# Padding of 64 bytes behind each row of the second weight matrix and each activation buffer, in a fused convolution and two-layer MLP on one core

## The chip, the core and the metric

The kernel runs on one core of a Trainium2 chip. The core has a matrix engine (TensorE, PE in the profile; PEld is its loading of weights), a vector engine (VectorE, DVE), a scalar engine (ScalarE, ACT), GpSimd (POOL) and a queue engine that starts transfers (SyncE, SP). They run side by side and wait for each other by semaphores. On-chip memory has 128 partitions, each of them a row of bytes; an address below means the byte within a partition. The metric is the device time of one execution in microseconds.

## The reference

```python
w = softmax(weight_gen, axis=-1)               # (4, 4096, 8 heads, 7 taps)
x = sum over k of w[..., k] * x_padded[s + k]  # causal, 7 taps, per head of 24 channels: (16384, 192)
h = x @ w_in                                   # (16384, 192) @ (192, 2048)
g = where(h >= 1, h, where(h <= -1, 0, (h + 1) ** 2 / 4))
out = g @ w_out                                # (16384, 2048) @ (2048, 192)
```

All inputs and the output are float32.

## The kernel before

The 16384 tokens are worked in 32 blocks of 512. For each block GpSimd and VectorE compute the convolution, and its result is turned so that channels lie on partitions. Then the block goes through the two matrix products: `steps` lists all (block, f) with f from 0 to 15, f being a slice of 128 of the 2048 hidden channels, and the main loop takes them two at a time (a pair, `w`), 8 pairs a block, 256 in all.

To keep float32 precision each operand of a product is held as a high and a low part in a reduced float32 type (F32R): `hc` and `hl` for the convolution's result, `whi` and `wlo` for the first matrix, `gh` and `gl` for the hidden values; `wo` holds for each f the high and then the low part of 128 rows of the second matrix, 192 columns each.

`gemm1_pair` computes a pair's two slices of h. `relu`, `square` (ScalarE) and `act_g` (VectorE) make g in place, and `split_g` (L398 to L405) writes gh on ScalarE (L403) and gl on VectorE (L404), each into one of six buffers of 512 words. `gemm2_part` follows two pairs later (`LAGP = 2`), in two parts per pair: it loads 128 columns of gh as weights and streams the 384 words of wo's row (high and low part together), then loads the same columns of gl and streams the 192 words of the high part alone (L432). Both products use the array as two halves of 64 rows each: the half is `h` in the code, and the matmul of one half runs beside that of the other. One turn of the loop so issues nine steps of the first product (each with both halves) and eight steps of the second, a step being gh and then gl for both halves.

The order on every engine is the order in which the code is written (`tc.manual_schedule()`). In the first pairs the weights are decoded and split: `high` (ScalarE, L352) and `low` (VectorE, L356) write `whi`, `wlo` and the two parts of `wo`, which `views` returns.

The built program places, in bytes within a partition: `whi` at 17408, `wlo` at 29696, `wo` at 41984 with a row every 1536, the gh buffers from 151552 on and the gl buffers from 163840 on with one every 2048, and behind them the convolution's `piece` buffers, the output buffers `osb` and the raw weights `r`. All starts of wo's rows, of gh, gl, hc, hl, whi and wlo, and of the 128-column slices of gh and gl that are loaded as weights, are multiples of 512. A `piece` has rows of 1024 bytes; its 128-column slices, which are loaded as weights where it is turned (L267), begin at 0, 256 and 512 within a row.

Of the kernel before, what the change touches and what calls it, by code (L numbers as in the profile page):

```python
# [11 lines left out]
F32R = mybir.dt.float32r  # L12
# [10 lines left out]
def kernel(  # L23
# [22 lines left out]
    P = 128  # L46
    B, S, D = x.shape
# [5 lines left out]
    NF = DFF // P  # L53
# [21 lines left out]
    const = ctx.enter_context(tc.tile_pool(name="const", bufs=1))  # L75
# [6 lines left out]
    gp = ctx.enter_context(tc.tile_pool(name="gp", bufs=6))  # L82
# [11 lines left out]
    warm = const.tile([P, 32], F32, tag="warm", name="warm")  # L94
    whi = const.tile([P, NF // 2, NC, P], F32R, tag="whi", name="whi")
    wlo = const.tile([P, NF // 2, NC, P], F32R, tag="wlo", name="wlo")
    wo = const.tile([P, NF, 2, D], F32R, tag="wo", name="wo")
    heads = [const.tile([P, (D // Q) * P + 2 * D + 0, 2], U16, tag=f"head{m}", name="head") for m in range(2)]

    def run(ops):  # L100
# [297 lines left out]

    def split_g(i):
        gv = h_t.pop(i)[:, 0:N]  # L400
        gh = gp.tile([P, 512], F32R, tag="gh", name="gh")
        gl = gp.tile([P, 512], F32R, tag="gl", name="gl")
        nc.scalar.activation(out=gh[:, 0:N], in_=gv, func=AF.Copy)  # L403
        nc.vector.tensor_tensor(out=gl[:, 0:N], in0=gv, in1=gh[:, 0:N].bitcast(F32), op=ALU.subtract)  # L404
        g_t[i] = (gh, gl)  # L405
# [125 lines left out]
    with tc.manual_schedule():  # L531
# [55 lines left out]
        def first_pairs():  # L587
# [26 lines left out]
            low(2, 1)  # L614
            act_g(1)
            split_g(0)
            relu(2)
            square(2)
            split_g(1)
            relu(3)  # L620
            square(3)
            act_g(2)
            act_g(3)
            split_g(2)
            split_g(3)
            cast_act(3, 0)
# [123 lines left out]
```

## Time and profile before

| | |
|---|---|
| time, median of 2 runs | 1147.0 us (1146.97 to 1147.03) |
| the profiled execution | 1147.49 us, span of its instructions 1145.6 us |
| TensorE matmul (PE) | 1130.8 us busy, 12885 instructions |
| TensorE weight load (PEld) | 1053.4 us busy |
| ScalarE (ACT) | 964.4 us busy |
| VectorE (DVE) | 833.7 us busy |
| GpSimd (POOL) | 792.3 us busy |
| mean granted clock of TensorE | 0.996 of full speed |

Matmuls are pipelined: the record of one lasts longer than the distance to the next, and the two halves overlap, so the distance between starts tells what one costs. In a timeline, records that follow each other with the same line and tiles are merged into one row with their count (x2: the two halves), the first one's start and the length to the last one's end.

### The profile page before, as it was taken

The page shows a single profiled execution, that of the slowest core. Times are in us where ns is not written, and L with a number is a line of the kernel's source. Part 1 is how long each engine was busy: PE and PEld are TensorE (multiplying, and loading weights), DVE is VectorE, ACT ScalarE, POOL GpSimd, SP SyncE. Part 2 cuts the span into 40 slices and gives each one's busy share as a digit, 9 for nine tenths or more (in the row PEclk, how much of TensorE's full clock was granted, in tenths as well). Part 3 has the DMA queues.
Part 4 walks back from the last instruction along what each step waited for, and adds up shares of the span by engine and source line. Part 5 has one row for each costly group of instructions (what it writes and reads, how often), then busy time and mean ns, then how long its engine had stood idle before and what let it go on. Part 6 is the DMA issues. An engine that isn't in the chain of part 4 may idle for free.

```text
span 1145.6 us, 32197 instructions
## 1 busy us (share of the span) xinstructions
PE 1130.8 (99%) x12885; PEld 1053.4 (92%) x12885; DVE 833.7 (73%) x1271; ACT 964.4 (84%) x1745; POOL 792.3 (69%) x511
## 2 busy tenths in 40 slices
PE   7999999999999999999999999999999999999998
PEld 5889899999999999999999999999999999999997
DVE  8887767777676777767777677776767777677765
ACT  5878888888888888888888888888888888888886
POOL 4697976786866688486685866778576784866310
PEclk9899999999999999999999999999999999999999
DMA  9422222121222222222121222222222122221100
GB/s 231 113 77 75 88 86 92 62 84 66 80 91 91 65 82 67 78 99 91 57 82 67 86 91 87 64 77 76 78 91 79 67 81 76 83 91 57 48 24 16
DMA packets 84053, 91.44 MB, mean 80 GB/s; under 512 B 5056, under 2 KB 75712, under 8 KB 83904
## 3 DMA queue, kind: packets, MB, share of 16 engines
q1 hardware_dynamic: 83904, 89.39, 24.4%
q8 instruction: 102, 1.67, 0.6%
q14 instruction: 47, 0.39, 0.1%
HBM read 64.99 MB, written 24.38 MB: 78 GB/s over the span
## 4 chain that ended last, share of the span: by engine, by line
PE 90%; ACT 4%; DVE 2%; POOL 2%; issue 1%; DMA 1%; SPq 0%; DVEq 0%; POOLq 0%; ACTq 0%
PE o L432 46%; PE psh L378 44%; ACT u L392 1%; ACT u L389 1%; POOL acc L189 1%; DVE psh L397 1%; ACT gh L403 1%; PE psx L267 1%; DMA x<-in_x_dram 1%; POOL pr L179 1%; DVE gl L404 0%; ACT hc L258 0%; DVE s L153 0%; DVE psw L340 0%; ACT whi L352 0%
## 5 line engine op out<-in xcount | busy, mean ns | idle before, releaser
L432 PE MATMUL o<-wo,gh 64*128 64x384 f32 x4096 | 616.5, 353 | 0.8 <-SPq L441 0.8
L397 DVE SCALAR_TENSOR_TENSOR psh<-u,psh 128x512 f32<-128x512 f32 x512 | 354.7, 696 | 284.9 <-ACT u L392 284.6
L432 PE MATMUL o<-wo,gl 64*128 64x192 f32 x4096 | 560.8, 247 | 0.0
L432 PEld LDWEIGHTS o<-wo,gh 64*128 64x128 f32 x4096 | 472.8, 184 | 9.0 <-SPq L441 1.0
L432 PEld LDWEIGHTS o<-wo,gl 64*128 64x128 f32 x4096 | 468.7, 188 | 5.5
L378 PE MATMUL psh<-hc,whi 64*128 64x512 f32 x1536 | 371.4, 397 | 4.2 <-DVE wlo L356 2.5
L389 ACT ACTIVATE u<-psh 128x512 f32<-128x512 f32 x512 | 301.2, 588 | 79.7 <-PE psh L378 78.5
L378 PE MATMUL psh<-hc,wlo 64*128 64x512 f32 x1536 | 364.5, 390 | 0.0
L378 PE MATMUL psh<-hl,whi 64*128 64x512 f32 x1536 | 363.3, 389 | 0.0
L404 DVE TENSOR_TENSOR gl<-psh,gh 128x512 fp32r<-128x512 f32 x512 | 345.8, 686 | 15.2 <-ACT gh L403 1.1
L403 ACT ACTIVATE gh<-psh 128x512 fp32r<-128x512 f32 x512 | 299.2, 592 | 66.1 <-DVE psh L397 66.1
L189 POOL TENSOR_TENSOR acc<-acc,pr 128x768 f32<-128x768 f32 x185 | 343.5, 1857 | 6.6 <-DVE head L331 2.9
L392 ACT ACTIVATE u<-u 128x512 f32<-128x512 f32 x512 | 324.2, 633 | 16.0
L179 POOL TENSOR_TENSOR pr<-x,w 128x768 f32<-128x768 f32 x186 | 286.6, 1549 | 7.0 <-DVE psw L340 7.0
L259 POOL TENSOR_TENSOR hl<-XT,hc 128x512 fp32r<-128x512 f32 x90 | 115.2, 1293 | 209.9 <-ACT hc L258 146.8
L378 PEld LDWEIGHTS psh<-hc,whi 64*128 64x128 f32 x1536 | 200.3, 185 | 24.4 <-DVE wlo L356 4.1
L378 PEld LDWEIGHTS psh<-hl,whi 64*128 64x128 f32 x1536 | 200.1, 185 | 23.7 <-DVE hl L259 0.3
L378 PEld LDWEIGHTS psh<-hc,wlo 64*128 64x128 f32 x1536 | 200.3, 186 | 15.8
L179 POOL TENSOR_TENSOR acc<-x,w 128x768 f32<-128x768 f32 x31 | 48.1, 1551 | 69.9 <-DVE w L155 68.0
L258 ACT ACTIVATE hc<-XT 128x512 fp32r<-128x512 f32 x90 | 55.5, 618 | 0.0
L284 DVE STREAM_TRANSPOSE T<-acc 128x768 f32<-128x768 f32 x30 | 50.3, 1678 | 0.7 <-POOL acc L189 0.5
L457 DVE SCALAR_TENSOR_TENSOR osb<-o,osb 128x384 f32<-128x384 f32 x64 | 32.7, 555 | 2.6 <-ACT osb L456 2.6
(44 smaller groups left out, 188.0 us busy)
## 6 DMA issues: line engine op xcount, KB each, us to landing
x<-in_x_dram SPq DMA_DIRECT2D x28, 960.0 KB
XT<-D SPq DMA_DIRECT2D x180, 128.0 KB
out_dram<-osb SPq DMA_DIRECT2D x31, 384.0 KB
D<-T SPq DMA_DIRECT2D x30, 384.0 KB
x<-in_x_dram SPq DMA_DIRECT2D x4, 945.0 KB
w<-in_weight_gen_dram SPq DMA_DIRECT2D x15, 224.0 KB
r<-in_moe_w_in_dram SPq DMA_DIRECT2D x16, 192.0 KB
r<-in_moe_w_out_dram SPq DMA_DIRECT2D x8, 384.0 KB
```

Of the source, the lines that this page charges most:

```text
L179: held(eng.tensor_tensor(out=t, in0=xtile[:, k:k + n, :].rearrange("p j (h g) -> p j h g", h=H), in1=wt[:, gi, :, :, k:k + 1].to_broadcast ...
L189: held(eng.tensor_tensor(out=o, in0=s, in1=t, op=ALU.add))
L258: ops.append(lambda c=c: nc.scalar.activation(out=hc[:, c], in_=src[c], func=AF.Copy))
L259: ops.append(lambda c=c: lows.append(engines[c].tensor_tensor(out=hl[:, c], in0=src[c], in1=hc[:, c].bitcast(F32), op=ALU.subtract)))
L284: lambda: nc.vector.transpose(out=T.rearrange("p b c j -> p b j c"), in_=acc.rearrange("p j (r b) -> p b j r", b=R)),
L378: nc.tensor.matmul(out=pair[h][:, 0:N], lhsT=l[rows, f // 2, (c + h) % NC if b < 2 else c], rhs=r[rows, c], start=(s == 0), stop=(s == len ...
L389: nc.scalar.activation(out=u_t[i], in_=h_t[i][:, 0:N], func=AF.Relu, scale=0.5 * UNIT, bias=0.5)
L392: nc.scalar.activation(out=u_t[i], in_=u_t[i], func=AF.Square, scale=UNIT ** -0.5)
L397: nc.vector.scalar_tensor_tensor(out=pv, in0=uv, scalar=1.0 / UNIT, in1=pv, op0=ALU.min, op1=ALU.max)
L403: nc.scalar.activation(out=gh[:, 0:N], in_=gv, func=AF.Copy)
L404: nc.vector.tensor_tensor(out=gl[:, 0:N], in0=gv, in1=gh[:, 0:N].bitcast(F32), op=ALU.subtract)
L432: mm = nc.tensor.matmul(out=o_t[b][turn][:, k, 0:cols], lhsT=g_t[i][l][rows, t * P:(t + 1) * P], rhs=wo[rows, f].rearrange("p s d -> p (s ...
```

## The change

wo gets rows of 400 words, of which the first 384 are used as before; gh and gl get buffers of 528 words, of which the first 512 are used.

```diff
-    wo = const.tile([P, NF, 2, D], F32R, tag="wo", name="wo")
+    wo = const.tile([P, NF, 2 * D + 16], F32R, tag="wo", name="wo")[:, :, 0:2 * D].rearrange("p f (s d) -> p f s d", s=2)
...
-        gh = gp.tile([P, 512], F32R, tag="gh", name="gh")
-        gl = gp.tile([P, 512], F32R, tag="gl", name="gl")
+        gh = gp.tile([P, 512 + 16], F32R, tag="gh", name="gh")[:, 0:512]
+        gl = gp.tile([P, 512 + 16], F32R, tag="gl", name="gl")[:, 0:512]
```

The built programs have the same instructions in the same order on every engine, with the same waits and the same element counts; they differ in addresses alone, and in the row distance in the access patterns of the sixteen instructions that write the two parts of wo. wo's rows are now 1600 bytes apart and begin at multiples of 64, the gh and gl buffers are 2112 bytes apart. Tiles behind wo move up by 1024 bytes, those behind gl by 1792, which puts `piece`, `osb` and `r` 256 bytes further within 512.

## Rows read from the trace of the kernel before

**Rows 1.** The page: span, and busy time of each engine with its share and instructions.
```profile
span 1145.6 us, 32197 instructions
PE 1130.8 (99%) x12885; PEld 1053.4 (92%) x12885; DVE 833.7 (73%) x1271; ACT 964.4 (84%) x1745; POOL 792.3 (69%) x511
```

**Rows 2.** Stretches by window: from:to, length, busy time per engine, clock, DMA.
```profile
400.00:600.00 200.00, 200.00 (x2312) 196.94 (x2311) 145.64 (x221) 171.52 (x310) 152.35 (x97) 1.00 0.24 79
600.00:800.00 200.00, 200.00 (x2310) 182.99 (x2308) 145.37 (x219) 171.43 (x310) 145.79 (x94) 1.00 0.23 77
```

**Rows 3.** Waits of PE, longest and shortest of eight: total us, times, longest.
```profile
PE psx L208 <- POOL ident L541: 2.7, 1, 2.7
...
PE psh L378 <- DVE gl L404: 0.4, 2, 0.3
```

**Rows 4.** Timeline of PE, one turn: start, length, line, operation, tiles, shape, count.
```profile
601.63 0.33 PE L432 MATMUL o<-wo,gh 64*128 64x384 f32 x2
601.80 0.25 PE L432 MATMUL o<-wo,gl 64*128 64x192 f32 x2
601.89 0.36 PE L432 MATMUL o<-wo,gh 64*128 64x384 f32 x2
602.09 0.25 PE L432 MATMUL o<-wo,gl 64*128 64x192 f32 x2
602.17 0.36 PE L432 MATMUL o<-wo,gh 64*128 64x384 f32 x2
...
603.88 0.41 PE L378 MATMUL psh<-hc,whi 64*128 64x512 f32 x2
604.13 0.40 PE L378 MATMUL psh<-hc,wlo 64*128 64x512 f32 x2
...
605.73 0.39 PE L378 MATMUL psh<-hl,whi 64*128 64x512 f32 x2
605.96 0.33 PE L432 MATMUL o<-wo,gh 64*128 64x384 f32 x2
```

**Rows 5.** Timeline of the weight loads in the same turn.
```profile
601.41 0.19 PEld L432 LDWEIGHTS o<-wo,gh 64*128 64x128 f32 x2
601.63 0.19 PEld L432 LDWEIGHTS o<-wo,gl 64*128 64x128 f32 x2
601.80 0.19 PEld L432 LDWEIGHTS o<-wo,gh 64*128 64x128 f32 x2
601.91 0.19 PEld L432 LDWEIGHTS o<-wo,gl 64*128 64x128 f32 x2
```

**Rows 6.** Timeline of PE, second product 100 us later, other rows and buffers.
```profile
701.14 0.33 PE L432 MATMUL o<-wo,gh 64*128 64x384 f32 x2
...
701.69 0.36 PE L432 MATMUL o<-wo,gh 64*128 64x384 f32 x2
701.88 0.25 PE L432 MATMUL o<-wo,gl 64*128 64x192 f32 x2
...
703.39 0.41 PE L378 MATMUL psh<-hc,whi 64*128 64x512 f32 x2
```

**Rows 7.** Line L432, all of it: duration ns minimum/median/maximum, first and last start.
```profile
L432 PEld LDWEIGHTS o<-wo,gh x4096: 182/184/332, 25.7 to 1140.0; 64*128 64x128 f32 x196
L432 PE MATMUL o<-wo,gh x4096: 329/355/576, 26.0 to 1140.2; 64*128 64x384 f32 x196
L432 PEld LDWEIGHTS o<-wo,gl x4096: 183/188/334, 26.0 to 1140.6; 64*128 64x128 f32 x196
L432 PE MATMUL o<-wo,gl x4096: 243/247/362, 26.1 to 1140.7; 64*128 64x192 f32 x196
```

**Rows 8.** Line L267, the turning of the pieces, in the same columns.
```profile
L267 PEld LDWEIGHTS psx<-ident,piece x72: 137/140/142, 9.1 to 58.9; 128*128 128x128 f32 x72
```

**Rows 9.** Lines L403, L404, L352 and L356, in the same columns.
```profile
L403 ACT ACTIVATE gh<-psh x512: 576/598/612, 23.4 to 1137.3; 128x512 fp32r<-128x512 f32 x171
L404 DVE TENSOR_TENSOR gl<-psh,gh x512: 634/685/722, 24.5 to 1138.0; 128x512 fp32r<-128x512 f32 x171
L352 ACT ACTIVATE whi<-psw x8: 485/490/492, 14.3 to 51.4; 128x384 fp32r<-128x384 f32 x8
L352 ACT ACTIVATE wo<-psw x8: 472/492/499, 19.7 to 51.8; 128x384 fp32r<-128x384 f32 x8
L356 DVE TENSOR_TENSOR wlo<-psw,whi x8: 495/558/559, 15.1 to 51.9; 128x384 fp32r<-128x384 f32 x8
L356 DVE TENSOR_TENSOR wo<-psw,wo x8: 547/549/558, 20.2 to 52.4; 128x384 fp32r<-128x384 f32 x8
```

**Rows 10.** Stretches of the start by window, columns as in rows 2.
```profile
6.50:30.40 23.90, 18.44 (x151) 14.37 (x149) 21.89 (x40) 15.85 (x33) 10.30 (x8) 1.00 1.05 241
30.40:37.30 6.90, 6.50 (x36) 5.58 (x38) 5.88 (x12) 5.68 (x12) 4.69 (x3) 0.51 1.08 218
37.30:60.00 22.70, 21.61 (x224) 18.42 (x223) 19.56 (x36) 19.92 (x40) 16.64 (x10) 1.00 0.18 59
```

## The prediction, made before the result was known

> **What bounds the kernel now.** I read the page first. TensorE is busy for 1130.8 of 1145.6 us, far more than ScalarE (964.4) or VectorE (833.7) [rows 1]. A busy share alone doesn't say that TensorE waits for nobody, so I went on to the stretches by window: from 400 to 600 and from 600 to 800 us it is busy for 200.00 of 200.00 us at a granted clock of 1.00, while ScalarE has work for 171.5 and VectorE for 145.5 of each 200 us [rows 2]. The waits say the same: TensorE's longest wait by total is 2.7 us, and its wait for gl, the last thing made before the second matmul, is 0.4 us in all, in two places [rows 3]. So from about 60 us to the end the time is the length of TensorE's own queue, and an edit counts only as far as it changes what TensorE does per instruction.
>
> The timeline of TensorE shows what one turn of the main loop is made of [rows 4]. A row stands for two matmuls, one per half of 64 rows, and the second half runs along with the first, so what one costs is the distance from one row's start to the next. The first product takes nine steps: from 603.88 to 605.96, 2.08 us, mostly 0.23 us each. The second takes eight steps of one gh and one gl: from 601.63 to 603.88, 2.25 us. The turn is 601.63 to 605.96, 4.33 us. There are 32 blocks x 8 pairs = 256 turns: 256 x 4.33 = 1108 us of the 1145.6, and the second product, the part that reads the changed buffers, holds 256 x 2.25 = 576 us of it, in 256 x 8 = 2048 steps.
>
> Inside a step there is one thing that is not arithmetic. The first gh of a turn takes 0.17 us (601.63 to 601.80), the next ones 0.20 (601.89 to 602.09). The weight loads tell why [rows 5]: the load for the first gh starts at 601.41, 0.22 us ahead of its matmul. The load for the second starts at 601.80 together with the matmul of gl, and the next load follows at 601.91, so that load lasted 0.11 us, but the gl matmul has only 0.09 us of work to hide it. The seven later steps are (603.88 - 601.89) / 7 = 0.284 us long against 0.17 + 0.09 = 0.26 for the first: 0.025 us in each of the seven are a wait for a weight load.
>
> **The change part by part.** No instruction is added, removed, reordered or given another wait; every shape is the old one. What is left is addresses. Before, wo's rows are 1536 bytes apart and the twelve gh and gl buffers 2048 bytes, and all of them, and every slice of 128 columns that is loaded as weights, begin at a multiple of 512 bytes. After, rows and buffers are 64 bytes further apart each, so their starts are spread over the multiples of 64; what lies behind gl moves too (the raw weights, the pieces of the convolution and the output buffers now begin 256 bytes off a multiple of 512). Each of four kinds of work could notice:
>
> 1. TensorE's reads of wo, gh and gl, 2048 steps. Does their time hang on the address? The trace has two tests. First, wo's sixteen rows, the six gh and six gl buffers and the four slices lie at different distances from each other in every turn, in steps of 512 bytes, and two turns 100 us apart with other rows and other buffers repeat each other: 703.39 - 701.14 = 2.25 us, with a gh in the middle at 701.88 - 701.69 = 0.19 us, as before within the rounding of the rows [rows 6]. Over the 4096 matmuls of a kind, the median record is 355 ns for gh and 247 for gl with minima of 329 and 243; the loads have a median of 184 and 188 ns and a minimum of 182 and 183 [rows 7]. Second, an operand that is 256 bytes off: the convolution's pieces are loaded as weights in slices that begin 0, 256 and 512 bytes into a 1024-byte row, and all 72 of those loads last 137 to 142 ns [rows 8]; a third of them begin 256 bytes off, and no group stands apart by more than 5 ns. A step of 64 bytes is not in the trace. From below: if the whole 0.025 us wait were a collision of the load with the streaming read, and the padding ended it, 7 x 256 x 0.025 = 45 us would go. From above: the spread between kinds of loads in rows 7 is 188 - 184 = 4 ns, and between the two ends of rows 8 5 ns; if a read that begins off a multiple of 512 paid 5 ns for the load and 5 for the streaming, that would be 2048 x 0.010 = 20 us. I take 0, because rows 6 and 8 are the nearest and neither shows a dependence. A further reason: a load walks through 512 bytes in 0.11 us while the matmul walks through 768 or 1536 bytes in 0.09 or 0.17, so the two streams slide past each other over every offset in each step, wherever they begin. A collision by address would be met in every step before and after.
>
> The Trainium skill ("TensorE: Matmul & The Clock Gate", section "LDWEIGHTS (loading the stationary operand)") gives a weight load by its columns alone, columns over 1.2 GHz: 107 ns for 128. The 0.11 us between the two loads of rows 5 agrees with it, and by that rule the 0.025 us wait is the length of the load and no padding can take it away. The same skill ("SBUF — State Buffer", section "Who interferes with whom") gives TensorE two independent read ports and knows of one contention alone, that of VectorE with GpSimd; by it the sum is 0 too, where the collision reading gives minus 45 us.
>
> 2. The writes of gh by ScalarE (median 598 ns, 576 to 612) and of gl by VectorE (685, 634 to 722) [rows 9]: the same element count, contiguous, in another place. They are hidden: ScalarE has 200 - 171.5 = 28.5 us free in 200, VectorE 54.5 [rows 2], which at 200 / 4.33 = 46 turns is 0.62 and 1.18 us in each turn. With two gh and two gl per turn, a gh would have to grow by 0.31 us and a gl by 0.59 before TensorE waited. Without that cover, 10 ns on each would be 512 x 0.010 = 5 us.
>
> 3. The splitting of the weights into wo's two parts, eight instructions on each engine in the first 53 us. Here the row distance stands in the access pattern (400 words for 384). Its nearest row is the same instruction on the first matrix, where the output is contiguous: 490 ns against 492 on ScalarE, 558 against 549 on VectorE [rows 9]. A jump between rows costs nothing that shows; 16 x 0.01 us = 0.2 us at the most. I take 0.
>
> 4. Transfers and other engines on the moved tiles: sizes, counts and queues are the same. In the loop nobody on TensorE's side waits for them [rows 3]. I take 0.
>
> The sum: 1145.6 us of span + 0, and the profiled execution's 1147.5 us is 1.9 more than its span. It lies 0.5 us above the median of the runs, so the prediction is the median: 1147.0 us.
>
> One thing can move without any cause in the change. From 30.4 to 37.3 us the granted clock is 0.51, the lower level of 1.2 GHz; TensorE was busy for 18.4 of the 23.9 us ahead of it and for 21.6 of the 22.7 behind it, at 1.00 on both sides [rows 10]. The stretch costs about half its length, 3.5 us. Whether it comes, and how often, hangs on the first 40 us, where transfers and decoding race. Lost or doubled, it makes 1143.5 or 1150.5.
>
> **The rivals.** *Collisions end.* The streaming read of wo and the load of gh or gl lie on the same offsets, and the spread ends the 0.025 us waits: 1147 - 45 = 1102 us. For it: the wait is there, it is in the very part that is padded, and all starts share one alignment. Against it: 0.11 us is also the load's length where it waits for nothing, and rows 6 and 8 know no offset. If half of the collisions went, it would be 1124 us, just 2%.
>
> *Reads off the old alignment are dearer.* Every load and every stream now runs over one more boundary of 512 bytes than before; at 10 ns a step that is 1147 + 20 = 1167 us. It decides from 23 us / 2048 = 11 ns per step on (4% of the 284 ns), in the second product alone; at half the price it would be 1157 us and still within 2%. Against it stands rows 8, where a load that crosses such a boundary lasts as long as the others.
>
> *The start goes another way.* The change leaves the loop alone and the stretch of lower clock is lost or doubled, by the 3.5 us above: 1143.5 or 1150.5 us. For it: those 6.9 us lie where TensorE still waits for others, so a small shift can move them. Against it: the two runs of before lie 0.06 us apart, so the start repeats itself. That the padding does nothing is no rival here but the forecast.
>
> **How the numbers follow.** No change beyond 3 us: 0.86. The start's slow clock lost, doubled or moved: 0.05 (1143.5 or 1150.5). Collisions end, wholly or partly: 0.05 (1102 to 1140, in over half of it by more than 2%). Dearer reads: 0.04 (1152 to 1185, half of it over 2%). 2% is about what a measurement of this kernel can tell from no change. From these: faster by over 2% 0.03, slower 0.02, within 2% 0.95. The range takes in the forecast and the clock's two ends: 1143.5 to 1150.5 us, which leaves out less than 2 in 10.
>
> **What would show it.** In the changed kernel's timeline of TensorE the steps of the second product should again be 0.28 to 0.29 us, with 0.17 for the first gh and 0.20 for the others, and a turn 4.33 us; TensorE should again be busy for 200.00 of 200.00 us. A gh of 0.17 us in the middle of a turn, or a gh record with a median near 330 ns, would show the collision reading right. Steps of 0.295 us or loads with a median above 188 ns would show the dearer reads. Loads as before with a different total would point to the first 60 us, and there to the stretch of lower clock. The prediction is wrong if either product's steps move by more than 1.7 ns (3.5 us / 2048).

## The result

The changed kernel takes 1154.8 us (1154.5 to 1155.2) where the kernel before takes 1147.0: a ratio of 1.0068, with a 95% interval of 1.0051 to 1.0084. It is slower by 7.8 us, 0.7%. That is within the 2% and outside the range of 1143.5 to 1150.5.

The page of the changed kernel (span, and busy time by engine, answering [rows 1]) and the stretches that answer [rows 2]:

```profile
span 1153.2 us, 32197 instructions
PE 1138.6 (99%) x12885; PEld 1063.9 (92%) x12885; DVE 833.7 (72%) x1271; ACT 965.3 (84%) x1745; POOL 792.7 (69%) x511
```
```profile
400.00:600.00 200.00, 200.00 (x2296) 193.80 (x2294) 144.72 (x218) 170.30 (x308) 151.43 (x97) 1.00 0.24 77
600.00:800.00 200.00, 200.00 (x2296) 182.24 (x2294) 142.94 (x217) 170.53 (x307) 142.87 (x92) 1.00 0.24 79
```

VectorE, ScalarE and GpSimd are busy for as long as before, to 1 us. TensorE is busy for 7.8 us longer, and in these stretches it is neither a wait nor the clock: in both it is busy for 200.00 of 200.00 us at 1.00, and gets through 2296 matmuls where it got through 2312 and 2310. On average a matmul takes a little longer.

How much, the timeline shows over six turns. These are the first row of the first product in each turn, and after two of them the first row of the second product (start, length, line, operation, tiles, shape, count), in the changed kernel:

```profile
602.04 0.42 PE L378 MATMUL psh<-hc,whi 64*128 64x512 f32 x2
604.12 0.34 PE L432 MATMUL o<-wo,gh 64*128 64x384 f32 x2
606.38 0.41 PE L378 MATMUL psh<-hc,whi 64*128 64x512 f32 x2
608.48 0.34 PE L432 MATMUL o<-wo,gh 64*128 64x384 f32 x2
610.75 0.42 PE L378 MATMUL psh<-hc,whi 64*128 64x512 f32 x2
...
615.10 0.42 PE L378 MATMUL psh<-hc,whi 64*128 64x512 f32 x2
...
619.47 0.42 PE L378 MATMUL psh<-hc,whi 64*128 64x512 f32 x2
...
623.85 0.41 PE L378 MATMUL psh<-hc,whi 64*128 64x512 f32 x2
...
628.19 0.42 PE L378 MATMUL psh<-hc,whi 64*128 64x512 f32 x2
```

and, of the kernel before, the row that stands six turns behind the 603.88 of [rows 4]:

```profile
629.84 0.41 PE L378 MATMUL psh<-hc,whi 64*128 64x512 f32 x2
```

Before, six turns took 629.84 - 603.88 = 25.96 us, 4.327 each. Now they take 628.19 - 602.04 = 26.15, 4.358 each, and they differ: 4.34, 4.37, 4.35, 4.37, 4.38, 4.34 us. The first product differs too: 604.12 - 602.04 = 2.08 us in one turn and 608.48 - 606.38 = 2.10 in the next, though the edit touches nothing that it reads.

The trace holds starts to the nanosecond. Taken over all turns, the lengths repeat every six turns: 4.352, 4.363, 4.382, 4.343, 4.344, 4.368 us, against 4.326 to 4.327 before, but for a few turns of either kernel that hold a wait. On average that is 32 ns more in a turn: 17 in the first product (2.093 us against 2.076) and 15 in the second (2.266 against 2.251). From the 18th turn to the last, the first product has 3.6 us more than before and the second 4.5, of which about 1.0 stands in a few turns that are longer by 0.1 to 0.8 us; the start of the kernel is 0.6 us shorter. 3.6 + 4.5 - 0.6 = 7.5 us.

Three rows of the whole trace of the changed kernel, in the columns of [rows 7], and the third of them as the kernel before has it:

```profile
L432 PEld LDWEIGHTS o<-wo,gh x4096: 182/184/323, 24.9 to 1147.6; 64*128 64x128 f32 x196
L432 PE MATMUL o<-wo,gh x4096: 330/356/443, 25.1 to 1147.8; 64*128 64x384 f32 x196
L378 PE MATMUL psh<-hc,whi x1536: 383/394/792, 14.9 to 1140.8; 64*128 64x512 f32 x192
```
```profile
L378 PE MATMUL psh<-hc,whi x1536: 383/386/792, 15.8 to 1133.3; 64*128 64x512 f32 x192
```

At L432 the medians hardly move: 184 ns as before for the load, 356 for 355. At L378 the matmul of hc and whi does move, from 386 to 394 ns. What a loss of some 2 ns a matmul comes to is told by the distance from start to start alone.

The waits of TensorE at L432 (total us, times, longest), and the one of them that lies in the longest of these turns, with the wait in brackets:

```profile
PE o L432 <- SPq L441: 1.7, 2, 1.1
```
```profile
950.62 0.45 PE L432 MATMUL o<-wo,gh 64*128 64x384 f32 x2 [0.52 <-SPq L441]
```

The other, of 1.1 us, lies at 27.8 us, where the kernel before has one of 0.8.

### The profile page after: what moved, and what is told of

The parts are those of the page before. It is cut to its first block, busy times and chain, and to the rows that moved or that the text cites. A ratio compares the mean times of both kernels' runs of the same rounds, so it can differ in the third digit from the quotient of the medians.

```text
span 1153.2 us, 32197 instructions
## 1 busy us (share of the span) xinstructions
PE 1138.6 (99%) x12885; PEld 1063.9 (92%) x12885; DVE 833.7 (72%) x1271; ACT 965.3 (84%) x1745; POOL 792.7 (69%) x511
## 4 chain that ended last, share of the span: by engine, by line
PE 92%; ACT 3%; DVE 2%; POOL 2%; issue 1%; DMA 0%; SPq 0%; DVEq 0%; POOLq 0%; ACTq 0%
PE o L432 47%; PE psh L378 45%; POOL acc L189 1%; ACT u L392 1%; PE psx L267 1%; ACT u L389 1%; ACT gh L403 1%; DVE psh L397 1%; POOL pr L179 1%; DMA x<-in_x_dram 0%; DVE gl L404 0%; DVE psw L340 0%; ACT whi L352 0%; ACT hc L258 0%; ACT wo L352 0%
## 5 line engine op out<-in xcount | busy, mean ns | idle before, releaser
L432 PE MATMUL o<-wo,gh 64*128 64x384 f32 x4096 | 613.8, 353 | 1.7 <-SPq L441 1.7
L432 PE MATMUL o<-wo,gl 64*128 64x192 f32 x4096 | 551.8, 248 | 0.0
L432 PEld LDWEIGHTS o<-wo,gh 64*128 64x128 f32 x4096 | 460.3, 184 | 9.9 <-SPq L441 2.6
L432 PEld LDWEIGHTS o<-wo,gl 64*128 64x128 f32 x4096 | 461.9, 187 | 6.5
L378 PE MATMUL psh<-hc,whi 64*128 64x512 f32 x1536 | 355.7, 400 | 3.9 <-DVE wlo L356 2.5
L404 DVE TENSOR_TENSOR gl<-psh,gh 128x512 fp32r<-128x512 f32 x512 | 345.7, 686 | 15.4 <-ACT gh L403 1.1
L403 ACT ACTIVATE gh<-psh 128x512 fp32r<-128x512 f32 x512 | 299.6, 593 | 65.5 <-DVE psh L397 65.5
L378 PE MATMUL psh<-hl,whi 64*128 64x512 f32 x1536 | 345.8, 390 | 0.0
L378 PE MATMUL psh<-hc,wlo 64*128 64x512 f32 x1536 | 345.2, 388 | 0.0
L378 PEld LDWEIGHTS psh<-hc,whi 64*128 64x128 f32 x1536 | 185.5, 184 | 22.8 <-DVE wlo L356 4.1
L378 PEld LDWEIGHTS psh<-hl,whi 64*128 64x128 f32 x1536 | 185.7, 184 | 22.6 <-DVE hl L259 0.3
L378 PEld LDWEIGHTS psh<-hc,wlo 64*128 64x128 f32 x1536 | 186.4, 186 | 14.4
```

Source lines behind the costliest of these rows:

```text
L378: nc.tensor.matmul(out=pair[h][:, 0:N], lhsT=l[rows, f // 2, (c + h) % NC if b < 2 else c], rhs=r[rows, c], start=(s == 0), stop=(s == len ...
L432: mm = nc.tensor.matmul(out=o_t[b][turn][:, k, 0:cols], lhsT=g_t[i][l][rows, t * P:(t + 1) * P], rhs=wo[rows, f].rearrange("p s d -> p (s ...
```

## The experiments

Theory A: the row that streams and the slice that is loaded as weights beside it are read at the same time, and what the pair costs depends on the offset between their addresses. Theory B: the tiles behind the padding moved, hc and hl among them, and that costs. Theory C: a stream that runs off its old alignment is dearer by itself. Every experiment leaves the order of all instructions and their waits as they are; only addresses differ. Lengths of a turn and of the two products are medians over the turns from the 24th on, from starts in each run's trace. Runs 5 to 12 were executed once each, and 14 executions of the kernel before spread from 1146.4 to 1148.2 us; so there the turns decide, and not the time.

| | turn, us | first product | second product | time, us | before, same chip |
|---|---|---|---|---|---|
| before | 4.327 | 2.076 | 2.251 | 1147.0 | |
| the change | 4.343 to 4.382, period 6 | 2.077 to 2.111 | 2.255 to 2.274 | 1154.8 | |
| 1: wo alone padded | 4.333 / 4.387 | 2.071 / 2.105 | 2.262 / 2.282 | 1154.5 | 1147.0 |
| 2: gh, gl alone padded | 4.348 / 4.380 / 4.338 | 2.076 / 2.103 / 2.073 | 2.273 / 2.277 / 2.265 | 1153.4 | 1147.0 |
| 3: other tiles moved, no padding | 4.327 | 2.076 | 2.251 | 1146.9 | 1147.0 |
| 4: gh, gl +64 bytes | 4.347 | 2.075 | 2.272 | 1151.7 | 1147.0 |
| 5: gh, gl +32 | 4.353 | 2.084 | 2.269 | 1151.7 | 1147.9 |
| 6: gh, gl +128 | 4.387 | 2.118 | 2.268 | 1160.0 | 1147.9 |
| 7: gh, gl +256 | 4.327 | 2.076 | 2.251 | 1148.1 | 1147.9 |
| 8: wo, gh, gl +64 | 4.353 | 2.104 | 2.249 | 1154.2 | 1147.9 |
| 9: everything +64 | 4.327 | 2.076 | 2.251 | 1148.9 | 1146.6 |
| 10: whi, wlo, hc, hl +64 | 4.340 | 2.088 | 2.252 | 1151.2 | 1146.6 |
| 11: hc, hl +64 | 4.353 | 2.102 | 2.251 | 1153.3 | 1146.6 |
| 12: 256 bytes behind each gh | 4.327 | 2.076 | 2.251 | 1146.1 | 1146.6 |

### 1 and 2: one half of the change each

Only wo's line of the diff:

```diff
-    wo = const.tile([P, NF, 2, D], F32R, tag="wo", name="wo")
+    wo = const.tile([P, NF, 2 * D + 16], F32R, tag="wo", name="wo")[:, :, 0:2 * D].rearrange("p f (s d) -> p f s d", s=2)
```

> Only wo's rows are padded (1600 bytes apart); gh and gl stand 2048 bytes apart at multiples of 512, and all tiles behind wo lie 1024 bytes higher, as in the changed kernel. Theory A (offset between the streamed row of wo and the loaded slice of gh or gl): about half of the loss, 1149 to 1153 us, and turns of two lengths that alternate, because wo's start moves by 128 bytes from turn to turn. Theory B (the tiles that moved, hc and hl among them): a loss of about 4 us, all of it in the first product, equal in every turn. Theory C (streaming from wo's padded rows is dearer by itself): the whole loss, 1155 us.

The ratio is 1.0066 (1.0051 to 1.0081). The timeline, in the rows that were shown for the changed kernel:

```profile
602.08 0.42 PE L378 MATMUL psh<-hc,whi 64*128 64x512 f32 x2
604.15 0.34 PE L432 MATMUL o<-wo,gh 64*128 64x384 f32 x2
606.42 0.42 PE L378 MATMUL psh<-hc,whi 64*128 64x512 f32 x2
608.52 0.35 PE L432 MATMUL o<-wo,gh 64*128 64x384 f32 x2
```

The first product takes 2.07 us in one turn and 2.10 in the next, and so on in turn: the two lengths that theory A expects. Theory C's 1155 is met in size, but not its shape: C, as it was put down, has the padded rows dearer by themselves, and so every turn alike.

Only the lines on gh and gl:

```diff
-        gh = gp.tile([P, 512], F32R, tag="gh", name="gh")
-        gl = gp.tile([P, 512], F32R, tag="gl", name="gl")
+        gh = gp.tile([P, 512 + 16], F32R, tag="gh", name="gh")[:, 0:512]
+        gl = gp.tile([P, 512 + 16], F32R, tag="gl", name="gl")[:, 0:512]
```

> Only the gh and gl buffers are padded (2112 bytes apart); wo and all tiles up to gh stand where they stood before. Theory A: about half of the loss, 1149 to 1153 us, in a pattern of three turns, because a turn uses two of six buffers. Theory B: hc and hl have not moved, so no loss in the first product, 1147 us. Theory C: 1147 us.

The ratio is 1.0057 (1.0042 to 1.0072):

```profile
601.52 0.48 PE L378 MATMUL psh<-hc,whi 64*128 64x512 f32 x2
...
605.90 0.48 PE L378 MATMUL psh<-hc,whi 64*128 64x512 f32 x2
...
610.24 0.48 PE L378 MATMUL psh<-hc,whi 64*128 64x512 f32 x2
...
614.59 0.48 PE L378 MATMUL psh<-hc,whi 64*128 64x512 f32 x2
```

4.38, 4.34, 4.35 us: three lengths, as A expects of six buffers used two at a time. Two and three make the six of the changed kernel. One thing goes beyond A: at 2112 bytes apart the first and the third pair of buffers stand alike modulo 256 bytes, the distance at which the price repeats (runs 7 and 12), and still no two of the three turns are alike. What came ahead of a turn counts too, which runs 8 and 10 show by themselves. B and C expected no loss here, and both fall with this run for the loss in it. A's size was off in both: each half costs not half but nearly the whole loss, and the two don't add up, 7.6 and 6.4 us alone, 7.8 together.

### 3: the other tiles moved, nothing padded

```diff
+    const.tile([P, 256], F32, tag="gap1", name="gap1")       # behind wo
+    gap2 = ctx.enter_context(tc.tile_pool(name="gap2", bufs=1))   # behind gl
+    gap2.tile([P, 192], F32, tag="gap2", name="gap2")
```

> Nothing is padded; an unused tile of 1024 bytes behind wo and one of 768 bytes behind gl put every other tile where it stands in the changed kernel, and wo's rows, gh and gl keep their distances and begin at multiples of 512. Theory A: no loss, 1147 us, turns of 4.327 us. Theory B: the first product longer by 16 ns a turn, 1151 us, or with the rest 1155. Theory C: 1147 us.

The ratio is 1.000 (0.999 to 1.0009):

```profile
602.57 0.41 PE L378 MATMUL psh<-hc,whi 64*128 64x512 f32 x2
...
628.53 0.41 PE L378 MATMUL psh<-hc,whi 64*128 64x512 f32 x2
```

Six turns in 25.96 us, as before. Theory B falls: hc, hl, piece, osb and the raw weights may lie where they lie in the changed kernel.

### 4 to 7: one offset for all steps

Nothing is padded between buffers; an unused tile ahead of the gh buffers moves all of gh and gl together, and a second one behind them fills up to 512 bytes.

```diff
+    gap1 = ctx.enter_context(tc.tile_pool(name="gap1", bufs=1))   # ahead of gh and gl: 64, 32, 128 or 256 bytes
     gp = ctx.enter_context(tc.tile_pool(name="gp", bufs=6))
+    gap2 = ctx.enter_context(tc.tile_pool(name="gap2", bufs=1))   # behind them: the rest of 512
...
```

> Nothing is padded between buffers; all gh and gl buffers together begin 64 bytes past a multiple of 512, wo stays at multiples of 512. So the offset between stream and load is the same 64 bytes in every step. Theory A: every turn has one and the same length, but another than 4.327 us, by -20 to +60 ns (1142 to 1162 us); a length between 4.32 and 4.33 in all turns would speak against it. Theory B and theory C: 1147 us.

The ratio is 1.0051 (1.0032 to 1.007):

```profile
600.22 0.41 PE L378 MATMUL psh<-hc,whi 64*128 64x512 f32 x2
602.29 0.34 PE L432 MATMUL o<-wo,gh 64*128 64x384 f32 x2
...
626.30 0.41 PE L378 MATMUL psh<-hc,whi 64*128 64x512 f32 x2
```

Six turns in 26.08 us, all 4.347. With one offset for all steps there is one length for all turns, and another than before.

The run also answers a rival that had no run of its own: that TensorE's reads are disturbed by ScalarE and VectorE, which write gh and gl meanwhile. In the traces before and here 1.1 of the 1.2 us per turn in which ScalarE writes gh, and 0.6 of VectorE's 1.4 us for gl, lie beside the first product. Here these writes have moved by 64 bytes against all that the first product reads, and it takes 2.075 us, as before.

> As the run with gh and gl 64 bytes past a multiple of 512, but 32 bytes. Theory A (each stream of wo meets the load of gh or gl that runs beside it, and their offset sets the price): all turns of one length, not 4.327 us; if the price grows with the offset, between 4.327 and 4.347 us. Rival A2 (it is enough to leave the multiples of 64, or of some larger step): 4.327 us or 4.347 us exactly.

> The same with 128 bytes. Theory A with a price that grows with the offset: above 4.347 us. Theory A with a price that repeats every 128 bytes: 4.327 us. In either case one length in all turns, and 2.075 us for the first product.

> The same with 256 bytes. In the changed kernel the turns repeat every 6, where wo's offset alone would repeat every 4 turns within 512 bytes and every 2 within 256: so the price should repeat every 256 bytes, and this kernel should have the 4.327 us turns of the kernel before and 1147 us. If it repeats only every 512 bytes or more: another length.

The first rows of the second product four turns apart, first with 32 bytes, then with 128, and those of the first product six turns apart with 256:

```profile
602.24 0.46 PE L432 MATMUL o<-wo,gh 64*128 64x384 f32 x2
...
619.65 0.46 PE L432 MATMUL o<-wo,gh 64*128 64x384 f32 x2
```
```profile
601.96 0.49 PE L432 MATMUL o<-wo,gh 64*128 64x384 f32 x2
...
619.51 0.49 PE L432 MATMUL o<-wo,gh 64*128 64x384 f32 x2
```
```profile
603.59 0.41 PE L378 MATMUL psh<-hc,whi 64*128 64x512 f32 x2
...
629.55 0.41 PE L378 MATMUL psh<-hc,whi 64*128 64x512 f32 x2
```

17.41 / 4 = 4.353 us, 17.55 / 4 = 4.387 us and 25.96 / 6 = 4.327 us. An offset of 256 bytes is as good as none, step by step; 128 is the dearest of those tried; 32 costs a little more than 64, so the price doesn't grow evenly with the offset, as I had expected. With 128 bytes 42 of the 60 ns fall into the first product, whose own operands didn't move: my 2.075 us for it were wrong. In the second product, whose loads did move, the three offsets cost nearly the same (18, 21 and 17 ns a turn for 32, 64 and 128 bytes); what sets the runs apart is the first product.

The rows of runs 5 and 6 are 0.46 and 0.49 us long where run 4 has 0.34. That is not the price. A merged row reaches from the start of one half to the end of the other, and here the second half starts 123 and 157 ns behind the first. The kernel before has such a lag too: 223 ns around 200 us, then 150, and 3 ns from the 125th turn on, with turns of 4.327 us at each of the three. The halves of run 6 are back in step later, and its turn is still 4.39 us (2.27 for the second product, 2.12 for the first). First a row of the kernel before in its early part, to set beside the 0.40 us of [rows 4], then run 6:

```profile
202.08 0.61 PE L378 MATMUL psh<-hc,wlo 64*128 64x512 f32 x2
```
```profile
1049.88 0.34 PE L432 MATMUL o<-wo,gh 64*128 64x384 f32 x2
...
1052.15 0.42 PE L378 MATMUL psh<-hc,whi 64*128 64x512 f32 x2
...
1054.27 0.33 PE L432 MATMUL o<-wo,gh 64*128 64x384 f32 x2
```

So halves that fall out of step are not the cause of the longer turns.

### 8 to 10: is it the place or the offset?

```diff
+    const.tile([P, 16], F32, tag="gap3", name="gap3")     # 8: ahead of wo, and the 64 bytes ahead of gh and gl as in 4
...
```

> wo's rows, gh and gl all begin 64 bytes past a multiple of 512, nothing is padded between them. Theory A, offset between stream and load alone: the second product as before, 2.251 us, turns of 4.327 us but for the two places where the products meet (up to 10 ns), 1147 to 1150 us. Rival: the position within 512 bytes counts by itself (a read that begins off the grid crosses one more boundary): 2.27 us or more for the second product, 1151 us or more.

```profile
601.51 0.43 PE L378 MATMUL psh<-hc,whi 64*128 64x512 f32 x2
603.62 0.34 PE L432 MATMUL o<-wo,gh 64*128 64x384 f32 x2
...
627.63 0.43 PE L378 MATMUL psh<-hc,whi 64*128 64x512 f32 x2
```

The second product, with all its operands 64 bytes off the old grid but none off another, is back at 2.249 us. The first, whose operands stand where they stood, takes 603.62 - 601.51 = 2.11 us. It isn't only the steps at the handover: the nine distances from start to start are on average 255, 232, 235, 229, 228, 234, 231, 231 and 230 ns against 252, 232, 231 and six of 227 before. My "up to 10 ns" at the two handovers was too small, and 1154.2 us lies outside my 1147 to 1150. It is a time that the rival allowed, but the rival has 2.27 us or more for the second product, and that is not so.

```diff
-    warm = const.tile([P, 32], F32, tag="warm", name="warm")
+    warm = const.tile([P, 48], F32, tag="warm", name="warm")     # 9: whi and all that lies behind it +64
```

> Every operand of both products (whi, wlo, hc, hl, wo, gh, gl) and all that lies behind begins 64 bytes past a multiple of 512; nothing is padded between them. Theory A (only offsets between operands count): turns of 4.327 us, 2.076 for the first product and 2.251 for the second, 1147 us. Rival (the place within 256 or 512 bytes counts by itself): a length above 4.34 us in all turns, 1150 us or more.

```profile
599.92 0.41 PE L378 MATMUL psh<-hc,whi 64*128 64x512 f32 x2
...
625.88 0.41 PE L378 MATMUL psh<-hc,whi 64*128 64x512 f32 x2
```

25.96 us for six turns: every operand begins off the old grid, and the loop's turn is that of before, to the nanosecond. What the single run has above 1147 us in its 1148.9 is not in the regular turns. This speaks against theory C and against the rival that the place itself counts, for the one place that was tried. What counts is the offset between operands.

```diff
+    gap5 = ctx.enter_context(tc.tile_pool(name="gap5", bufs=1))   # 10: 64 bytes ahead of hc and hl, warm as in 9, wo, gh and gl back at multiples of 512
...
```

> whi, wlo, hc and hl begin 64 bytes past a multiple of 512, wo, gh and gl at multiples: within each product all offsets are equal, and only where one product hands over to the other do stream and load differ, by 64 bytes the other way round than in the run with wo, gh and gl moved. Theory A with a rhythm that is set at the handover and lasts: one of the products is longer through all of its steps, 10 to 30 ns in the turn, 1149 to 1155 us. Rival (only the step that itself has the offset pays): at most the two steps at the handovers differ, 4.327 to 4.340 us, all other steps as in the kernel before.

```profile
600.85 0.42 PE L378 MATMUL psh<-hc,whi 64*128 64x512 f32 x2
...
626.88 0.42 PE L378 MATMUL psh<-hc,whi 64*128 64x512 f32 x2
```

26.03 / 6 = 4.338, by all turns 4.340 us. The offsets differ only where one product hands over to the other, and the first product is longer by 12 ns. Its steps are 254, 236, 229, 232, 231, 227, 226, 227, 226 ns: here the disturbance lasts for five steps and is then gone. It is longer than the one step at the handover, and not through all of the steps as in run 8: between what the two theories expected. An unequal handover into the first product is not the only way, though: in run 6 wo and whi, which meet where the second product hands over to the first, both stand at multiples of 512, and the first product is the longest of all.

### 11 and 12: other operands, and a harmless padding

> Only hc and hl, the streams of the first product, begin 64 bytes past a multiple of 512; its weights whi and wlo and the whole second product stand at multiples. Theory A as a matter of any stream against any load, not of wo and g: the first product changes in its steps, by 10 ns or more in a turn to either side of 2.076 us, 1143 to 1155 us. Rival (it is the second product's tiles alone): 4.327 us, 1147 us.

The edit is the 64 bytes ahead of hc and hl of run 10 alone.

```profile
600.78 0.42 PE L378 MATMUL psh<-hc,whi 64*128 64x512 f32 x1
...
602.88 0.42 PE L432 MATMUL o<-wo,gh 64*128 64x384 f32 x2
```

2.10 us for the first product, 2.251 for the second (4.353 in all). wo, gh and gl have no special part in it: the streamed operand against the loaded one does the same in the first product. Within it the streams' distance to each other is as before, and so is that of the loads; only stream and load moved apart.

```diff
-        gh = gp.tile([P, 512], F32R, tag="gh", name="gh")
+        gh = gp.tile([P, 512 + 64], F32R, tag="gh", name="gh")[:, 0:512]
```

> The change's own edit on gh, but with 64 words (256 bytes) behind each buffer in place of 16: buffers 2304 bytes apart that begin at multiples of 256. Theory A with a price that repeats every 256 bytes: turns of 4.327 us in all, 1147 us. Rival (a padded buffer costs by itself, through its distance to the next): a pattern of three turns as in the run with 16 words.

```profile
602.13 0.42 PE L378 MATMUL psh<-hc,whi 64*128 64x512 f32 x2
...
628.09 0.42 PE L378 MATMUL psh<-hc,whi 64*128 64x512 f32 x2
```

25.96 us, and 1146.1 us in all beside 1146.6 for the kernel before. A padded buffer costs nothing by itself: 16 words behind each gh and gl cost (run 2), 64 behind each gh don't.

No layout that was run has turns below 4.327 us, so there was no faster version to run. The shortest pieces seen, 2.071 us for the first product in run 1 and 2.249 for the second in run 8, stand in turns that are longer as a whole.

## Why the prediction was wrong

**The frame held.** TensorE's own queue is the time: 200.00 of 200.00 us busy, no new wait of weight (0.5 us in the one turn above), ScalarE and VectorE as long as before (parts 2 and 3 of the change at nothing), the moved tiles free (part 4, run 3). The start became shorter by 0.6 us. The loop's first matmul already starts 0.9 us earlier (14.9 against 15.8 us), ahead of the stretch of low clock; that stretch is about half as long, with a mean of 0.75 in the window where [rows 10] had 0.51. The same window of the changed kernel and then of run 12, where it is missing altogether:

```profile
30.40:37.30 6.90, 6.90 (x59) 6.07 (x60) 5.85 (x12) 5.75 (x12) 3.99 (x4) 0.75 1.08 205
```
```profile
30.40:37.30 6.90, 6.71 (x65) 5.64 (x66) 6.41 (x13) 6.14 (x12) 4.54 (x4) 1.00 1.11 201
```

The 3.5 us that the prediction put on this stretch, and from which it took both ends of its range, are not borne out: run 12, without it and with turns of 4.327 us, took 1146.1 us, 0.9 below the 1147.0. Of the 14 executions of the kernel before, the four with a mean clock of 1.000 took 1146.4 to 1147.6 us, the six with 0.996 to 0.998 took 1146.8 to 1147.9.

**The step that failed is part 1, the price of 0 for the 2048 steps.** It rested on three arguments. Rows 6 compare turns whose addresses differ by multiples of 512 bytes. Rows 8 compare loads that differ by 256, and do it by the length of a load's record; at L432 that record has a median of 184 ns in the changed kernel as before, so it doesn't tell the price. Runs 7 and 12 show that the price repeats every 256 bytes: both tests looked exactly at distances that cost nothing. The text said that a step of 64 bytes was not in the trace, and then took the value of the nearest rows for it. The third argument, that the two streams slide past each other over every offset and would meet a collision "in every step before and after", is wrong as such: runs 4 to 6 have other lengths with one fixed offset, so where the two begin does count. What the runs showed in place of the 0: a stream and a load that run together cost more or less by the offset between their starts, here 32 ns a turn, on average 1.9 ns for each of the nine steps of the first product and of the eight of the second.

**The size lay within the bounds of the working, but not in the range.** The upper bound was 10 ns a step, 20 us. Over the steps of the second product it was 15 ns / 8 = 1.9 ns. The rival "reads off the old alignment are dearer", at 0.04, had the right sign, and the measured 1154.8 us lies in its 1152 to 1185. That is a hit of the number alone: run 9 has every read off the old alignment and its turns lose nothing. Its signs would have missed the loss, too: the steps of the second product are 2.266 / 8 = 0.283 us and not 0.295, and no median of a load rose above 188 ns.

**It put the price in the second product alone.** Over half of what a turn loses, 17 of 32 ns, lies in the first product, whose own streams and loads kept their offsets (runs 6, 8 and 10 show such a carrying over). "Either product's steps move by more than 1.7 ns" was named as what would make the prediction wrong; it was just that, 1.9 ns in both products at once.

**The rival of collisions that end** goes too: the wait at a gh is still there. In the changed kernel, behind its 604.12, the first gh of a turn takes 0.17 us (604.12 to 604.29) and the next 0.19 (604.38 to 604.57), where [rows 4] have 0.17 and 0.20:

```profile
604.29 0.25 PE L432 MATMUL o<-wo,gl 64*128 64x192 f32 x2
604.38 0.35 PE L432 MATMUL o<-wo,gh 64*128 64x384 f32 x2
604.57 0.25 PE L432 MATMUL o<-wo,gl 64*128 64x192 f32 x2
```

The Trainium skill ("TensorE: Matmul & The Clock Gate", section "LDWEIGHTS (loading the stationary operand)") gives a load by its columns alone, and by it no padding could take this wait away; that the wait stayed agrees. The other rule of the Trainium skill that was cited, two independent read ports of TensorE ("SBUF — State Buffer", section "Who interferes with whom"), leaves no room for an offset to count: by it alone every run of the table would have turns of 4.327 us. The measurement says otherwise, by up to 60 ns a turn. With one offset moved and nothing else, load and stream together take longer; which of the two is held up, the runs don't show.

**What stays open.** What it is in the memory that stream and load share, and why a disturbance lasts for nine steps of the first product in run 8 and for five in run 10, no run shows; nor what lengthens the first product of run 6. Offsets other than 32, 64, 128 and 256 bytes were not run by themselves.

## What to carry to other kernels

Where TensorE is the bound, these runs speak for laying out operands that are streamed and loaded at the same time at equal offsets modulo 256 bytes, and for a padding that is a multiple of 256 bytes: 16 words behind wo's rows, gh and gl cost this kernel 0.7%, 64 words behind gh nothing. A trace is evidence about addresses only at the distances it holds; before a price of nothing is taken from rows that agree, ask whether they could have differed. A loss of 2 ns a matmul is invisible in the busy share (99% in both kernels) and all but invisible in the median records, and plain in the distance from turn to turn.

## What the runs showed of the hardware that I had not expected

The loop's length hangs on the offset between the streamed operand and the weights that are being loaded, with a period of 256 bytes: 4.327 us at 0 and 256, 4.353 at 32, 4.347 at 64, 4.387 at 128. The place itself didn't count: 4.327 with everything moved by 64. And the disturbance outlives its cause: in run 8 a first product whose own operands hadn't moved took 2.104 us instead of 2.076 beside a second product that had moved as a whole and was itself no longer. How far the two halves run apart, on the other hand, 3 or 223 ns, changes nothing in the length of a turn.
